# Gate times up on GpSimd instead of VectorE, with the rounding of h later in ScalarE's order

## The chip, the cores and the metric

The kernel runs on one core of one Trainium2 chip. The metric is the device time of one execution in microseconds. A core has TensorE (PE in the profile; its weight loads are PEld), VectorE (DVE), ScalarE (ACT), GpSimd (POOL) and SyncE (SP), which issues most DMAs. Each engine takes its own instructions in order; between engines they wait on semaphores.

## The reference

x is 2048 rows by 576 columns. After a layer norm, two branches work on the same normed rows and are multiplied:

```python
xn = _layernorm(x, axis=-1)
s = _A_ref(xn, A_wqkv, A_wo)              # attention with 32 heads of 18 columns, times wo
g = jnp.einsum("bsd,df->bsf", x, w_gate)  # in _B_ref, with xn for x; f has 4608 columns
u = jnp.einsum("bsd,df->bsf", x, w_up)
h = g * u
return jnp.einsum("bsf,fd->bsd", h, w_down)
return x + s * silu(B)                    # the end of reference(): B is that last product
```

## The kernel before, in words

All matrices are float32. A value that goes into a matmul is split into a rounded part (fp32r) and the rest, and a product is made of three matmuls (high by high, low by high, high by low). The split is two instructions: ScalarE copies the value with rounding, and GpSimd subtracts the rounded part from it.

A first stage (about 195 us) norms the rows and makes queries, keys and values. The main stage (about 195 to 2501 us) runs attention and the gated unit side by side. The last stage multiplies the two branches and applies wo.

In the main stage the gated unit's work is cut into 72 units: 4 blocks of 512 rows by 18 blocks of 256 columns of f. A unit has two halves j, so n = 2u + j counts 144 halves. TensorE runs two streams at once on the two halves of its rows: stream 0 makes up of half n (27 matmuls of 512 columns, L678), stream 1 makes gate of half n. Both accumulate in one of the four PSUM banks called pg. Up's end (`up_end`, L683) is a ScalarE copy of the bank to the tile `us`, of which there are two buffers. Gate's end (`gate_end`, L685 to L697) multiplies on VectorE the gate's bank with `us`, in place (L690), asks for the weights of half n + 2, rounds the product on ScalarE (L693) and subtracts on GpSimd (L694); this fills the tile `hs`. `turn_round` (L710) swaps the halves of `hs` into `hx` by two DMAs, issued by SyncE at the end of the unit before. Then the unit is multiplied with w_down (L720, 96 matmuls of 288 columns), and VectorE adds the banks to sums (L748).

Attention is put between these matmuls. An `a` item (L596) is a matmul of scores into one of two banks pa, of which VectorE takes row maxima (L598); there are 64 of them a head. After the 64th, VectorE folds the maxima and turns them (L604 to L613: `max_fold`, `max_rows`), and GpSimd issues four DMAs with them (L618), which stand in GpSimd's order ahead of whatever is put in later. A `b` item (L628) is the matmul of transposed scores into one of two banks pb, followed by an exponential on ScalarE (L630). Every seven row blocks there is a `visit`, in which TensorE does only the products with the values (L639, some 6 us). When a head is complete, `finish` (L651 to L659) divides: VectorE transposes into the tile `tp` (one buffer), scales it (L655) and transposes back, and GpSimd issues four DMAs with the result.

The order of all instructions is made when the program is built, by a planner written into the kernel (`order`, from L1100 on): it keeps a clock for each TensorE stream, and one "free from" time for VectorE, ScalarE and GpSimd, and puts in the item whose bank is free and whose goal is due. `engine(name, start, taken)` books time on an engine. GpSimd's DMA issues are not booked. For the end of a gate the planner books VectorE for 0.60 us, then ScalarE for 0.535 and GpSimd for 1.29.

Of the kernel before, what the change touches and what calls it, by code (L numbers as in the profile page):

```python
# [20 lines left out]
FT = mybir.dt.float32  # L21
FR = mybir.dt.float32r
I32 = mybir.dt.int32
AF = mybir.ActivationFunctionType
OP = mybir.AluOpType
# [15 lines left out]
def kernel(  # L41
# [10 lines left out]
    nc = tc.nc  # L52
# [116 lines left out]
    def g_get(n):  # L169

        if n == 2 * len(units):
            u = n // 2 - 1
            dw[u] = wpool.tile([128, 2, 2, 2, HALF], FR, name="wdl", tag="wgu", bufs=2)
            nc.sync.dma_start(dw[u].bitcast(FT), swd[columns_of(u)])
            ddone.add(u)
        if n >= 2 * len(units):
            return
        f = 2 * columns_of(n // 2) + n % 2
        if n > 1 and n // 2 % NF2 == 0:
            gw[n] = gw[n - 2]  # L180
            gdone.add(n)
            return
        w = gw[n] = g_tile()
        if n >= 2 * NF2:
            nc.sync.dma_start(w.bitcast(FT), swg[f])
            gdone.add(n)
            return
        if n not in graw:
            ready(gdone, n - 2)
        raw = graw.pop(n)  # L190

        def piece(b):
            nc.scalar.activation(w[:, b:b + 3, :], raw[:, b:b + 3, :], AF.Copy)  # L193
            nc.gpsimd.tensor_tensor(w[:, 9 + b:12 + b, :], raw[:, b:b + 3, :], w[:, b:b + 3, :].bitcast(FT),  # L194
                                    op=OP.subtract)

        def end():
            gdone.add(n)
            nc.sync.dma_start(swg[f], w.bitcast(FT))
            g_load(n + 2)  # L200

        chores.extend([(piece, (b,)) for b in (0, 3, 6)] + [(end, ())])
# [353 lines left out]
    n = 8  # L556
# [21 lines left out]
    with ExitStack() as mid:  # L578
# [106 lines left out]
        def gate_end(n, ps):  # L685
            u, j = divmod(n, 2)
            if j == 0:
                hs[u] = gp.tile([128, 2, 2, 512], FR, name="hs", bufs=2)
            h32 = us.pop(n)
            nc.vector.tensor_tensor(h32, ps, h32, op=OP.mult)  # L690
            g_get(n + 2)
            hj = hs[u][:, j]
            nc.scalar.activation(hj[:, 0, :], h32, AF.Copy)  # L693
            nc.gpsimd.tensor_tensor(hj[:, 1, :], h32, hj[:, 0, :].bitcast(FT), op=OP.subtract)  # L694
            if u == 0 and j or u == len(units) - 1:
                turn_round(u, j)

        hx = {}

        def turn_round(u, j):  # L700

            if u == len(units) - 1:
                if j == 0:
                    hx[u] = accp.tile([128, 2, 2, 512], FR, name="hxl", tag="acc")
                js = slice(j, j + 1)
            else:
                hx[u] = gp.tile([128, 2, 2, 512], FR, name="hx", bufs=1)
                js = slice(0, 2)
            for r in range(2):
                nc.sync.dma_start(hx[u][half[r], js].bitcast(FT), hs[u][half[1 - r], js].bitcast(FT))  # L710
# [2 lines left out]

        def down_start(r, u):
            ready(ddone, u)
            return bank("g", 1, slots[r])

        def down_op(r, u, s, ps, n):
# [129 lines left out]
        def stream(r):  # L848

            for u in range(len(units) + 1):  # L850
                for n in (2 * u, 2 * u + 1):
                    if u == len(units):
                        break
                    c, q = units[u]
                    box = []
                    for k in range(len(TERMS)):
                        def work(n=n, k=k, box=box, c=c, q=q):
                            if k == 0:
                                box.append(gu_start(r, n))
                            gu_op(r, n, box[0], k)  # L860
                            if q == NF2 - 1 and n % 2 and k % 3 == 2 and c < NCH - 1:
                                x_block(c + 1, k // 3, (64 * r,))
                                there["x", c + 1, k // 3, r] = moved(clk[r] + 0.5, 0.262)
                            if k == len(TERMS) - 1:
                                (gate_end if r else up_end)(n, box[0])
                                if r and n == 2 * len(units) - 1:
                                    wo_load()
                                    moved(max(clk), 1.47)
                        end = (("DVE", 0.60) if r else ("ACT", 0.50)) if k == len(TERMS) - 1 else None
                        yield LONG, k == 0, work, end, ("g", n, k)  # L870
                for s in range(4):
                    if not u:
                        break
                    box = []
                    for k in range(len(DTERMS)):
                        def work(s=s, k=k, box=box, u=u - 1):
                            if k == 0:
                                box.append(down_start(r, u))
                            down_op(r, u, s, box[0], k)
                            if k == len(DTERMS) - 1:  # L880
                                down_end(r, u, s, box[0])
                        end = ("DVE", 0.365) if k == len(DTERMS) - 1 else None
                        yield SHORT, k == 0, work, end, ("d", u - 1, 12 * s + k)
# [227 lines left out]
        def order():  # L1111
# [4 lines left out]
            wait = None  # L1116
            while any(heads) or na < TOTAL or nb < TOTAL or due:
                now = max(clk)
                small(now)
                if nb == TOTAL and not lo:  # L1120
                    begin()
# [28 lines left out]
                if can and (at <= clk[r] + 0.01 and (goal <= clk[r] or blocked) or op is None and (at <= clk[r] or not held)):  # L1150
                    clk[r] = max(clk[r], at)
                    score(r)
                elif op is not None:
                    length, first, work, end, (kind, n, k) = op
                    if first:
                        clk[r] = max(clk[r], next_free("g"))
                        slots[r] = banks["g"].index(next_free("g"))
                        banks["g"][slots[r]] = 1e9
                    work()
                    lands = issue(r, length)  # L1160
                    gone[r] += length
                    if end:
                        done = engine(end[0], lands, end[1])
                        banks["g"][slots[r]] = done + EARLY
                        if kind == "d":
                            if k == 47:
                                parts.setdefault(n, []).append(clk[r])
                                if len(parts[n]) == 2:
                                    downed[n] = moved(max(parts[n]) + 0.3, 1.18) if (n + 1) % NF2 and n + 2 < len(units) else 0.0
                                    if n + 2 < len(units):  # L1170
                                        there["h", n + 1] = moved(max(parts[n]) + 1.0, 1.05)
                        elif r == 0:
                            upped[n] = done
                        else:
                            gated[n] = done
                            fin = engine("ACT", done + 0.05, 0.535)
                            fin = engine("POOL", fin + 0.05, 1.29)
                            loaded[n] = moved(done - 0.4, 1.18) if (n // 2 + 1) % NF2 else 0.0
                            if n // 2 == len(units) - 1:
                                there["h", n // 2] = moved(fin, 0.524)  # L1180
                            elif n == 1:
                                there["h", 0] = moved(fin, 1.05)
                            for _ in range(2):
                                hot = n + 2 >= 2 * NF2 and n % (2 * NF2) in (34, 35, 0) and n + 2 < 2 * len(units)
                                for want in stacks:
                                    if hot and (want[0] is load_pair or n % (2 * NF2) == 2 * NF2 - 1):
                                        continue
                                    stacks.remove(want)
                                    send(want, fin + 1.4)
                                    break  # L1190
                    heads[r] = next(feeds[r], None)
                else:
                    clk[r] = max(clk[r] + 0.05, min(clk[1 - r] + 0.01, clk[r] + 0.3))
# [120 lines left out]
```

## Time and profile before

| | |
|---|---|
| median of 3 runs | 2570.12 us (2569.12 to 2572.28) |
| the profiled execution | 2571.43 us, of which its span is 2569.4 us |
| TensorE busy | 2547.8 us, 99% of the span |
| VectorE busy | 1933.2 us, 75% |
| ScalarE busy | 1467.1 us, 57% |
| GpSimd busy | 594.8 us, 23% |
| chain that ended last | 95% TensorE, 3% DMA, 1% VectorE |

The span runs from the first to the last instruction; the 2.0 us beyond it lie around the program. The chain is followed back from the last instruction, at each step to what released it. Times are microseconds unless marked as ns.

### The profile page before, as it was taken

Reading aid. Unit: us, or ns where it says so; the run is one execution under the profiler, and the core shown is the slowest. Engines: PE = TensorE matmul, PEld = TensorE weight load, DVE = VectorE, ACT = ScalarE, POOL = GpSimd, SP = SyncE. Lnnn points to the kernel's source line nnn. Section 1 sums busy time; section 2 is a strip of 40 time slices with the busy share of each in tenths; the row PEclk is TensorE's granted clock in tenths of the full one; section 3 lists DMA queues with packets and bytes.
Section 4 is the critical chain, followed back from the end, with each engine's and each line's share of the span. In section 5 each row is a group of like instructions: output and inputs, shape, how many; then the busy total and the mean of one; then the engine's idle time right before and its main releaser. Section 6 shows DMA issues by size and latency. Waiting matters only on the chain.

```text
span 2569.4 us, 59203 instructions
## 1 busy us (share of the span) xinstructions
PE 2547.8 (99%) x24360; PEld 2111.1 (82%) x24360; DVE 1933.2 (75%) x3377; ACT 1467.1 (57%) x2688; POOL 594.8 (23%) x663
## 2 busy tenths in 40 slices
PE   8999999999999999999999999999999999999999
PEld 7899888878878888877888888777888877888878
DVE  6208778777778898777778888777888887778437
ACT  5222666666756665555665665555665655556651
POOL 3214434434421111111111111111111111111125
PEclk9999999999999999999999999999999999999999
DMA  7799988888886666665686656665686666654567
GB/s 243 235 284 278 263 226 225 232 225 220 221 206 186 176 182 177 175 179 155 179 197 173 179 175 184 176 170 154 179 204 166 180 184 176 175 174 146 159 189 248
DMA packets 195898, 504.58 MB, mean 196 GB/s; under 512 B 58112, under 2 KB 116352, under 8 KB 156588
## 3 DMA queue, kind: packets, MB, share of 16 engines
q1 hardware_dynamic: 185676, 489.05, 68.6%
q0 software_dynamic: 9952, 11.74, 1.7%
q8 instruction: 192, 3.15, 0.6%
q14 instruction: 78, 0.64, 0.1%
HBM read 312.21 MB, written 107.61 MB: 163 GB/s over the span
## 4 chain that ended last, share of the span: by engine, by line
PE 95%; DMA 3%; DVE 1%; SPq 0%; ACT 0%; issue 0%; POOL 0%; ACTq 0%; DVEq 0%
PE pg L678 34%; PE pg L639 18%; PE pg L720 16%; PE pa L596 12%; PE pb L628 8%; PE pg L402 2%; PE pa L348 2%; PE pb L348 2%; PE pg L1244 1%; DMA hx<-hs 1%; PE pb L1244 1%; PE pa L1244 1%; DMA sqk<-hl 0%; DMA ring<-sqk 0%; DMA xc<-sx 0%; DMA o<-sot 0%
## 5 line engine op out<-in xcount | busy, mean ns | idle before, releaser
L598 DVE TENSOR_REDUCE mx<-pa 128x1 f32<-128x512 f32 x2048 | 1367.1, 686 | 223.6 <-PE pa L596 104.8
L630 ACT ACTIVATE pt<-pb 128x512 f32<-128x512 f32 x2048 | 1161.9, 598 | 534.8 <-PE pb L628 465.5
L678 PE MATMUL pg<-xc,wgu 64*128 64x512 f32 x7776 | 1366.1, 388 | 0.7 <-DMA xc<-sx 0.5
L678 PEld LDWEIGHTS pg<-xc,wgu 64*128 64x128 f32 x7776 | 1051.7, 184 | 41.6 <-DMA xc<-sx 1.2
L628 PE MATMUL pb<-pair,ring 64*128 64x512 f32 x1997 | 777.4, 395 | 1.5 <-DMA ring<-sqk 1.5
L596 PE MATMUL pa<-pair,ring 64*128 64x512 f32 x2006 | 776.9, 393 | 1.8 <-DVE mx L598 1.8
L720 PE MATMUL pg<-wd,hs 64*128 64x288 f32 x3408 | 523.4, 292 | 0.0
L720 PE MATMUL pg<-wd,hx 64*128 64x288 f32 x3408 | 515.2, 292 | 2.4 <-DMA hx<-hs 2.4
L694 POOL TENSOR_TENSOR hs<-us,hs 128x512 fp32r<-128x512 f32 x144 | 186.2, 1293 | 1320.3 <-ACT hs L693 1285.6
L720 PEld LDWEIGHTS pg<-wd,hs 64*128 64x128 f32 x3408 | 459.8, 185 | 4.0 <-DVE acc L748 0.2
L720 PEld LDWEIGHTS pg<-wd,hx 64*128 64x128 f32 x3408 | 453.4, 185 | 6.5 <-DMA hx<-hs 3.0
L639 PE MATMUL pg<-pt,vt 128*32 128x512 f32 x4096 | 454.8, 594 | 0.7 <-DVE acc L748 0.6
L596 PEld LDWEIGHTS pa<-pair,ring 64*128 64x128 f32 x2006 | 364.3, 184 | 69.8 <-issue 52.8
L628 PEld LDWEIGHTS pb<-pair,ring 64*128 64x128 f32 x1997 | 362.5, 184 | 8.7 <-issue 1.9
L639 PEld LDWEIGHTS pg<-pt,vt 128*32 128x32 f32 x4096 | 125.5, 110 | 284.0 <-issue 278.9
L748 DVE TENSOR_TENSOR acc<-acc,pg 128x288 f32<-128x288 f32 x544 | 233.0, 443 | 22.4 <-PE pg L720 21.4
L645 DVE TENSOR_TENSOR oc<-oc,pg 128x512 f32<-128x512 f32 x69 | 47.1, 683 | 220.4 <-PE pg L639 213.7
L693 ACT ACTIVATE hs<-us 128x512 fp32r<-128x512 f32 x144 | 91.0, 632 | 151.0 <-DVE us L690 149.7
L194 POOL TENSOR_TENSOR wgu<-wraw,wgu 128x384 fp32r<-128x384 f32 x108 | 108.6, 1017 | 97.1 <-ACT wgu L193 84.6
L643 ACT ACTIVATE oc<-pg 128x512 f32<-128x512 f32 x32 | 19.2, 598 | 185.0 <-PE pg L639 179.0
L690 DVE TENSOR_TENSOR us<-pg,us 128x512 f32<-128x512 f32 x144 | 98.2, 682 | 26.9 <-PE pg L678 15.7
L618 POOL DMA_DIRECT2D pair<-mt x128 | 77.8, 613 | 166.4 <-DVE mt L613 162.3
(141 smaller groups left out, 1359.0 us busy)
## 6 DMA issues: line engine op xcount, KB each, us to landing
wgu<-swg SPq DMA_DIRECT2D x102, 1152.0 KB
hx<-hs SPq DMA_DIRECT2D x142, 512.0 KB
wd<-swd SPq DMA_DIRECT2D x50, 1152.0 KB
swg<-wgu SPq DMA_DIRECT2D x36, 1152.0 KB
pair<-sqk SPq DMA_DIRECT2D x192, 144.0 KB
ring<-sqk SPq DMA_DIRECT2D x384, 72.0 KB
swd<-wd SPq DMA_DIRECT2D x18, 1152.0 KB
sqk<-hl SPq DMA_DIRECT2D x32, 512.0 KB
```

Source lines behind the costliest of these rows:

```text
L194: nc.gpsimd.tensor_tensor(w[:, 9 + b:12 + b, :], raw[:, b:b + 3, :], w[:, b:b + 3, :].bitcast(FT), op=OP.subtract)
L348: nc.tensor.matmul(p, wq[b, a], xcs[c][:, e, :], start=n == 0, stop=n == len(PAIRS) - 1)
L596: nc.tensor.matmul(p, q[rows, t * 128:(t + 1) * 128], k[rows, c * 512:(c + 1) * 512], start=True, stop=True)
L598: nc.vector.tensor_reduce(mx[h][:, t, c:c + 1], p, axis=AX.X, op=OP.max)
L628: nc.tensor.matmul(p, k[rows, t * 128:(t + 1) * 128], q[rows, c * 512:(c + 1) * 512], start=True, stop=True)
L630: nc.scalar.activation(pt[t, c], p, AF.Exp, scale=scale)
L639: nc.tensor.matmul(p[32 * c:32 * c + 32, :], vt[h // 2][:, t, 6 * (h % 2):6 * (h % 2) + 32], pt[t, c], start=t == ts[0], stop=t == ts[-1])
L678: nc.tensor.matmul(ps, gw[n][half[r], a, :], xg[i][half[r], e, :], start=k == 0, stop=k == len(TERMS) - 1)
L690: nc.vector.tensor_tensor(h32, ps, h32, op=OP.mult)
L694: nc.gpsimd.tensor_tensor(hj[:, 1, :], h32, hj[:, 0, :].bitcast(FT), op=OP.subtract)
L720: nc.tensor.matmul(ps[:, 0:HALF], (hx if k else hs)[u][half[r], j, a, s * 128:(s + 1) * 128], dw[u][half[r], k, j, e, :], start=n == 0, st ...
L748: nc.vector.tensor_tensor(a, a, ps[:, 0:HALF], op=OP.add)
```

## The change

For 132 of the 144 halves (`by_pool`: 8 <= n < 140, and not after the attention has ended) the product of gate and up is no longer one VectorE instruction. ScalarE copies the gate's bank to a tile `gs`, which shares the single buffer of `tp`; GpSimd multiplies `us` by `gs` in place. The two instructions of the split of h move to `h_split`. It is not put in at once but kept in a list, `halves`, with the time of the gate's end plus 2.6 us. The planner puts it in when that time has come, GpSimd will be free within 0.2 us and ScalarE within 0.3 us by its books. `settle` puts it in at the latest ahead of `turn_round` of its unit. The planner books the gate's end on ScalarE (0.50 us) instead of VectorE and the product on GpSimd (1.25 us). The time `fin`, from which loads of keys and queries may be sent, is the end of the product plus 2.0 us in place of the end of the subtraction.

```diff
             h32 = us.pop(n)
-            nc.vector.tensor_tensor(h32, ps, h32, op=OP.mult)
+            if by_pool(n):
+                gs = mp.tile([128, 512], FT, name="gs", tag="tp", bufs=1)
+                nc.scalar.activation(gs, ps, AF.Copy)
+                nc.gpsimd.tensor_tensor(h32, h32, gs, op=OP.mult)
+            else:
+                nc.vector.tensor_tensor(h32, ps, h32, op=OP.mult)
             g_get(n + 2)
+            if by_pool(n):
+                halves.append((max(clk) + 2.6, n, h32))
+            else:
+                h_split(n, h32)
+
+        halves = []
+
+        def by_pool(n):
+            return 8 <= n < 2 * len(units) - 4 and not fin
+
+        def h_split(n, h32):
+            u, j = divmod(n, 2)
             hj = hs[u][:, j]
             nc.scalar.activation(hj[:, 0, :], h32, AF.Copy)
             nc.gpsimd.tensor_tensor(hj[:, 1, :], h32, hj[:, 0, :].bitcast(FT), op=OP.subtract)
...
+        def settle(u):
+            while halves and halves[0][1] <= 2 * u + 1:
+                h_split(*halves.pop(0)[1:])
+
         def turn_round(u, j):
+            if u < len(units) - 1:
+                settle(u)
...
-                        end = (("DVE", 0.60) if r else ("ACT", 0.50)) if k == len(TERMS) - 1 else None
+                        end = (("DVE", 0.60) if r and not by_pool(n) else ("ACT", 0.50)) if k == len(TERMS) - 1 else None
...
+                if halves and halves[0][0] <= now and free["POOL"] <= now + 0.2 and free["ACT"] <= now + 0.3:
+                    h_split(*halves.pop(0)[1:])
+                    engine("POOL", engine("ACT", now, 0.535) + 0.05, 1.29)
...
-                            fin = engine("ACT", done + 0.05, 0.535)
-                            fin = engine("POOL", fin + 0.05, 1.29)
+                            if by_pool(n):
+                                fin = engine("POOL", done + 0.05, 1.25) + 2.0
+                            else:
+                                fin = engine("ACT", done + 0.05, 0.535)
+                                fin = engine("POOL", fin + 0.05, 1.29)
```

## Rows read from the trace of the kernel before

**Rows 1.** The page's busy times: engine, busy us, share of the span, instructions.

```profile
PE 2547.8 (99%) x24360; PEld 2111.1 (82%) x24360; DVE 1933.2 (75%) x3377; ACT 1467.1 (57%) x2688; POOL 594.8 (23%) x663
```

**Rows 2.** Busy times by stretch, 294 to 2430 us: stretch, length, engines, granted clock, DMA.

```profile
294.00:700.00 406.00, 405.80 (x4036) 330.23 (x4034) 315.00 (x551) 274.24 (x527) 167.86 (x169) 1.00 0.87 228
...
sum 2136.00, PE 2131.99 PEld 1740.48 DVE 1710.88 ACT 1305.72 POOL 452.25; mean PE 426.40 PEld 348.10 DVE 342.18 ACT 261.14 POOL 90.45
```

**Rows 3.** Waits of TensorE, 294 to 2430 us: waiter, releaser, total us, times, longest.

```profile
PE pb L628 <- DMA ring<-sqk: 1.5, 1, 1.5
PE pa L596 <- DVE mx L598: 1.0, 2, 0.5
PEld pa L596 <- DVE mx L598: 2.5, 4, 0.9
PEld pb L628 <- ACT pt L630: 0.8, 4, 0.2
```

**Rows 4.** Groups of instructions, 294 to 2430 us: count, busy us, mean ns, idle before.

```profile
L690 DVE TENSOR_TENSOR us<-pg,us 128x512 f32<-128x512 f32 x132 | 90.0, 682 | 8.1 <-PE pg L678 7.5
L683 ACT ACTIVATE us<-pg 128x512 f32<-128x512 f32 x131 | 78.3, 598 | 6.1 <-PE pg L678 3.8 <-PE pb L628 0.6
L693 ACT ACTIVATE hs<-us 128x512 fp32r<-128x512 f32 x132 | 83.4, 632 | 125.1 <-DVE us L690 123.9 <-DMA hx<-hs 0.6 <-DMA ring<-sqk 0.6
L694 POOL TENSOR_TENSOR hs<-us,hs 128x512 fp32r<-128x512 f32 x132 | 170.6, 1293 | 1220.8 <-ACT hs L693 1192.4 <-DMA ring<-sqk 15.1 <-DMA draw<-in_B_w_down_dram 7.8
```

**Rows 5.** Timeline of a head's end, 1014 to 1022 us: start, us, engine, operation.

```profile
1015.38 0.68 DVE L690 TENSOR_TENSOR us<-pg,us 128x512 f32<-128x512 f32 x1
1016.81 1.29 POOL L694 TENSOR_TENSOR hs<-us,hs 128x512 fp32r<-128x512 f32 x1 [11.82 <-ACT hs L693]
1016.95 1.18 DVE L610 TENSOR_SCALAR mm<-m 128x16 fp32r<-128x16 f32 x1
1019.22 0.50 PE L596 MATMUL pa<-pair,ring 64*128 64x512 f32 x1 [0.51 <-DVE mx L598]
```

**Rows 6.** L610's shortest, median, longest in ns; its first and last long instance.

```profile
L610 DVE TENSOR_SCALAR mm<-m x32: 174/174/1187, 247.6 to 2405.9; 128x16 fp32r<-128x16 f32 x32
...
462.84 0.59 DVE L610 TENSOR_SCALAR mm<-m 128x16 fp32r<-128x16 f32 x1
...
2055.36 1.19 DVE L610 TENSOR_SCALAR mm<-m 128x16 fp32r<-128x16 f32 x1
```

**Rows 7.** Timelines of GpSimd behind a head's end: first, middle and last case.

```profile
390.03 2.38 POOL L618 DMA_DIRECT2D pair<-mt  x4 [4.43 <-DVE mt L613]
390.22 0.68 DVE L690 TENSOR_TENSOR us<-pg,us 128x512 f32<-128x512 f32 x1
...
1503.86 0.66 DVE L690 TENSOR_TENSOR us<-pg,us 128x512 f32<-128x512 f32 x1
1504.23 2.44 POOL L618 DMA_DIRECT2D pair<-mt  x4 [13.88 <-DVE mt L613]
...
2198.00 2.44 POOL L618 DMA_DIRECT2D pair<-mt  x4 [9.66 <-DVE mt L613]
2198.56 0.68 DVE L690 TENSOR_TENSOR us<-pg,us 128x512 f32<-128x512 f32 x1
```

**Rows 8.** Timeline of pb's matmuls and exponentials, 1503 to 1507 us.

```profile
1503.00 0.39 PE L628 MATMUL pb<-pair,ring 64*128 64x512 f32 x1
1505.09 1.07 ACT L630 ACTIVATE pt<-pb 128x512 f32<-128x512 f32 x2
1505.94 0.39 PE L628 MATMUL pb<-pair,ring 64*128 64x512 f32 x1
1506.37 1.09 ACT L630 ACTIVATE pt<-pb 128x512 f32<-128x512 f32 x2 [0.21 <-PE pb L628]
```

**Rows 9.** Timeline of the unit with least time between subtraction and turn.

```profile
2200.45 1.29 POOL L694 TENSOR_TENSOR hs<-us,hs 128x512 fp32r<-128x512 f32 x1
2206.43 1.11 SPq L710 DMA_DIRECT2D hx<-hs  x2
```

More of the change, by code (lines that the diff above doesn't have):

```diff
@@ L715, in down_start @@
             ready(ddone, u)
+            settle(u)
             return bank("g", 1, slots[r])
```

## The prediction

> **What bounds the kernel now.** I read the page's busy times first: TensorE is busy 2547.8 of 2569.4 us, at 99%, against 75% for VectorE [rows 1]. The change acts only while halves 8 to 139 are made, and the 132 products that it moves all lie between 294 and 2430 us [rows 4]. So I cut the span by stretches: from 294 to 2430 us TensorE is busy 2131.99 of 2136.00 us idle for 4.0 us, and the granted clock in the stretches is 1.00, the higher of its two levels (2.4 GHz) [rows 2]. VectorE has 425 us free there (2136.00 less 1710.88), ScalarE 830. Neither is a bound in the sense of busy time; each matters only where TensorE comes to a bank that it has not yet emptied. The list of TensorE's waits prices that: 1.0 us of TensorE's idle time ended with VectorE's row maxima, 1.5 us with a DMA of keys, and the loads of weights ahead of an a item waited 2.5 us in four places for the maxima. For ScalarE's exponentials they waited 0.8 us in all [rows 3]. That is the whole of what a lighter VectorE can give back. Idle time is not all, since one of the two streams can stand while the other goes on, so I allow twice the idle time as the most that there is to win, 8 us.
>
> **What the change takes from VectorE.** 132 products of 682 ns, 90.0 us of busy time [rows 4]. In the middle of the stage they cost TensorE nothing, since the maxima behind them have their place in the order. They cost something at one kind of place. At 1015.38 us the product ran, the subtraction of that half held GpSimd from 1016.81 to 1018.10, and VectorE's tiny L610 took 1.18 us from 1016.95 on, ending when GpSimd ended. The next maxima stood behind it, and TensorE stood 0.51 us ahead of an a item at 1019.22 [rows 5]. L610 has a median of 174 ns and a longest of 1187 [rows 6]. There are three such long ones inside this stretch, the first at 462.84, the last at 2055.36 us [rows 6]; at all three a half's subtraction ran on GpSimd, and the waits of rows 3 for the maxima lie there. The loss at one such place is 0.9 us at most, by the longest wait of a weight load [rows 3]; I take 0.7, together 2.1 us.
>
> The Trainium skill has a rule for this, and it speaks against the change: "SBUF — State Buffer", section "Who interferes with whom", says that GpSimd and VectorE share a pair of ports, held for a whole instruction, and that a VectorE instruction of the tensor_scalar kind, or one with two operands in SBUF, waits until GpSimd's is done. Row and rule agree (1.18 us against 0.17). By the rule alone, without a look at where the locked instructions stand, more GpSimd work means more such waits, and never fewer.
>
> Now the count after the change. A half takes 16.2 us (2136 us over 132), and GpSimd's tensor work on it goes from one instruction of 1.29 us to two [rows 4], so a head's end meets one in 16% of the cases instead of 8%: of 31 head ends in place of about 2.5 (three were seen) about 5. The mean length of a block is half an instruction, 0.65 us, and what TensorE loses is less by about 0.3, as at the three seen. Without the product's 0.68 us in VectorE's queue at the same place I take 0.4 us each, 2.0 us in all against 2.1 now. The term is **0.0 us**; its bounds are -2.1 (no such place is left) and 5 x 0.9 - 2.1 = +2.4. The scaling in `finish`, which has two operands in SBUF, stands in visits, where TensorE needs no maxima: nothing.
>
> **What it adds to ScalarE.** 132 copies from a bank, at 598 ns by the same copy of up's bank [rows 4], 78.9 us, which lie in the 830 us that ScalarE has free. The copy empties the gate's bank in 0.6 us instead of 0.68, and two of the four pg banks are in use by the streams, so the bank is nobody's wait. What goes away on ScalarE is the stand ahead of L693: 123.9 us before 132 roundings, 0.94 us each, in which the exponentials queue behind it [rows 4]. TensorE's order was made knowing it, and TensorE waited 0.8 us for exponentials altogether [rows 3], so its end gives at most **0.8 us**; I count nothing.
>
> **What it adds to GpSimd.** 132 products; by the subtraction of the same shape 1293 ns each, 170.7 us, in the 1684 us that GpSimd has free (2136.00 less 452.25) [rows 2, 4]. The product has two operands like the subtraction, so between bounds of 0.6 us (half) and 1.3 I take the subtraction's. Early on GpSimd also splits the weights: from 294 to 700 us it is busy 167.86 of 406 us, and 25 products raise that by 32 us to half [rows 2]. The planner books both; free.
>
> **Where the planner's books are wrong.** Rounding is put into ScalarE's order 2.6 us after the gate's end at the earliest. Matmul to copy takes some 0.4 us (an item's start to the start of what reads it, 1505.94 to 1506.37 [rows 8]), the copy 0.6, the product 1.29, the hand-overs 0.1: the product is there at 2.4 us. But GpSimd's queue is in order, and the four DMA issues of a head's end, 2.44 us together [rows 7], are not booked. Where a half ends just behind a head, the product stands behind them, and ScalarE stands at the rounding, with all exponentials behind it, at a place where TensorE's order does not know it. Today only the subtraction waits there, and nobody waits for it soon. I looked for products that come behind a head's last a item and would be ready (0.75 us after L690's start) ahead of the end of the four issues: there are 8 in the stretch, the first at 390.22 us (ready 390.97, issues done 392.41: 1.44 late), the middle one 1503.86 (2.06 late), the last 2198.56 (1.13 late) [rows 7]; the eight come to 10.7 us. What of such a delay reaches TensorE? An item takes the bank of the item two before it. The item at 1505.94 takes that of 1503.00, whose exponential, the first of the two from 1505.09 on, ended at about 1505.63 (half of 1.07): 0.3 us to spare [rows 8]. Items follow each other by about 0.9 us, so the first exponential behind a rounding comes on average 0.45 us later, and 0.2 us lie between 2.4 and 2.6. A delay of 1.34 us (10.7 over 8) leaves 1.34 - 0.3 - 0.45 - 0.2 = 0.4 us: 8 x 0.4, about **+3 us**. Bounds: 0, as the wait of 0.94 us at every half costs nothing today [rows 3, 4], and 10.7 + 8 x 0.2 (the copy can start earlier than L690 did) = +12. I take the value nearer the lower end since the rows of a stand at this very place are there.
>
> **What is moved.** The split comes 1.5 to 3 us later. The turn of `hs` by SyncE stands behind it: the least time from the end of a subtraction (2201.74) to the issue of its turn (2206.43) is 4.7 us [rows 9], so SyncE's queue, with the loads of keys and weights behind the turn, does not stand longer. `settle` puts the rounding in ahead of the turn at the latest. The buffer of `us` is taken again two halves later, over 15 us. `gs` shares a buffer with `tp`: a gate's copy can wait for a `finish`, or a `finish` for a product, up to 2.5 us, but `finish` lies in visits, ahead of which VectorE has nothing of TensorE's next items. **0 us**, bound +1. That planned times of loads move by 1.3 us (`fin`) can make a wait like the 1.5 us for keys [rows 3] come or go: 0, from -2 to +3.
>
> **Sum.** The profiled execution took 2571.43 us, 1.3 more than the median of 2570.12; I forecast against the median. 0.0 (locks) + 3 (roundings) - 0.5 (half of the possible gain on ScalarE, rounded) + 0 = +2.5: **2572.5 us**, inside the 0.2% (5.1 us) that a measurement of this kernel can tell from no change. Its own range is 2567 to 2575.
>
> **Rivals.** *ScalarE held by late products, slower.* As above, but nearly the whole delay reaches TensorE because the items come in dense rows behind a head's end: 8 x 1.2, about +10, 2580 us. It decides from 5.1 us on, that is if the eight lose 0.65 us each. For it: ScalarE is in order, and the spare of a bank is only 0.3 us [rows 8]. Against it: 0.8 us of waits now, with ScalarE standing at every half [rows 3, 4]. 0.19.
> *The lock, slower.* More GpSimd instructions hit L610, or L611 behind it, than the 5 of the count, since two of them now follow a gate. To be slower by 5.1 us it takes (5.1 + 2.1) / 0.9 = 8 of 31 head ends at the highest price; at ten, 10 x 0.9 - 2.1 = +7, 2577 us. For it: rows 5. Against it: 8 is far from 5 when all must be the dearest. By the skill's rule above this would be the way the time goes. 0.05.
> *VectorE's relief, faster.* All three head ends, ScalarE's 0.8 us and the wait for keys go, and the streams' one-sided stands with them: 2.1 + 0.8 + 1.5 + 2, about -6, 2564 us. For it: each is seen once. Against it: it needs all of them, and nothing new. 0.06.
> *The product isn't moved, or the splits fall back to the turn.* Then TensorE's waits stay as they are, 2570 us; it counts with no change, 0.02.
>
> **How the numbers follow.** The forecast has 0.68 and the last rival 0.02: no change 0.70; slower 0.19 + 0.05 = 0.24; faster 0.06. The range leaves out half of the faster case and about a third of the slower cases: 2566 to 2580.
>
> **What would show it.** L690 falls to 12 instructions, a ScalarE copy of a gate's bank to `gs` of about 0.6 us and a GpSimd product of about 1.29 us come in 132 times; VectorE's busy time falls by 90 us, ScalarE's rises by 79, GpSimd's by 171; TensorE's stays within 3 us of 2547.8. ScalarE's waits ahead of the rounding change their releaser from VectorE to GpSimd, and only those behind a head's end are long. L610 has about five long instances. The prediction is wrong if TensorE waits over 5 us for exponentials, if the turn waits for GpSimd, or if the products run other than 1.3 us.

## The result and the profile after

The changed kernel takes 2575.61 us in the median of 22 runs, the kernel before 2571.77 in as many beside it: a ratio of 1.0015, with a 95% interval of 1.0009 to 1.0022. That is 3.8 us slower, and within the 5.1 us that the prediction took for no change. The forecast was +2.4 us against the median shown then. As will be seen, the sum came out near the truth because a loss twice as large as counted met gains that were not counted.

The profiled execution took 2575.07 us with a span of 2573.3. Its busy times, to be read beside [rows 1]:

```profile
PE 2544.1 (99%) x24360; PEld 2106.5 (82%) x24360; DVE 1871.6 (73%) x3245; ACT 1526.7 (59%) x2820; POOL 766.0 (30%) x795
```

The work was moved as told: VectorE has 132 instructions fewer, ScalarE and GpSimd 132 more. VectorE's busy time fell by 62 us and not by 90, and ScalarE's rose by 60 and not by 79: busy time is a union, and instructions that follow each other closely overlap at their ends, so one that is taken out or put in counts for less than its own length (the lengths of VectorE's instructions, added up, fell by 84 us). GpSimd's rose by 171.

The groups of the gate's end, from 294 to 2434 us (columns as in [rows 4]):

```profile
L693 POOL TENSOR_TENSOR us<-us,gs 128x512 f32<-128x512 f32 x132 | 172.2, 1305 | 978.0 <-ACT gs L692 958.3 <-DMA swd<-wd 8.3 <-DMA draw<-in_B_w_down_dram 8.2
L711 POOL TENSOR_TENSOR hs<-us,hs 128x512 fp32r<-128x512 f32 x132 | 170.4, 1291 | 185.7 <-ACT hs L710 177.4 <-PE pa L596 2.7 <-PE pg L678 2.5
L710 ACT ACTIVATE hs<-us 128x512 fp32r<-128x512 f32 x132 | 82.8, 627 | 16.7 <-POOL us L693 16.6
L692 ACT ACTIVATE gs<-pg 128x512 f32<-128x512 f32 x131 | 78.4, 598 | 7.4 <-PE pg L678 1.8 <-PE pa L596 0.2 <-PE pg L744 0.2
```

The product takes 1305 ns on GpSimd (682 on VectorE before), the copy 598. ScalarE's stand ahead of the rounding is 16.7 us instead of 125.1 [rows 4]: it is seven times smaller. But see who pays. These are the waits of TensorE in the same stretch, to be read beside [rows 3]:

```profile
PE pb L628 <- ACT pt L630: 5.2, 5, 1.5
PE pb L628 <- DMA ring<-sqk: 0.8, 1, 0.8
PE pa L596 <- DVE mx L598: 0.6, 1, 0.6
```

Waits for exponentials, which were no wait of TensorE's own before, are 5.2 us in five places; waits for row maxima fell from 1.0 to 0.6, those for keys from 1.5 to 0.8. Four of the five are 1.84, 1.84, 1.35 and 1.37 us from one matmul's start to the next, at 951.6, 1504.9, 1648.8 and 2202.0 us, each just behind a head's end. One of them in the timeline of the changed kernel (start, us, engine, operation, idle before and who ended it):

```profile
1501.11 0.59 ACT L692 ACTIVATE gs<-pg 128x512 f32<-128x512 f32 x1
...
1505.54 0.63 ACT L710 ACTIVATE hs<-us 128x512 fp32r<-128x512 f32 x1 [2.29 <-POOL us L693]
1506.08 1.76 ACT L630 ACTIVATE pt<-pb 128x512 f32<-128x512 f32 x3
...
1501.76 2.44 POOL L618 DMA_DIRECT2D pair<-mt  x4 [12.79 <-DVE mt L613]
1504.21 1.30 POOL L693 TENSOR_TENSOR us<-us,gs 128x512 f32<-128x512 f32 x1
...
1506.71 0.49 PE L628 MATMUL pb<-pair,ring 64*128 64x512 f32 x1 [1.45 <-ACT pt L630]
```

The gate's copy is done at 1501.70. The product could begin, but GpSimd is issuing the head's four DMAs until 1504.20. ScalarE comes to the rounding at 1503.26 and stands 2.29 us, three exponentials queue behind it, and TensorE stands for 1.45 us at a pb item. This is the half with the L690 at 1503.86 of [rows 7].

### The profile page after: what moved, and what is told of

Its sections match the earlier page's. It is cut to its first block, busy times and chain, and to the rows that moved or that the text cites. A ratio compares the mean times of both kernels' runs of the same rounds, so it can differ in the third digit from the quotient of the medians.

```text
span 2573.3 us, 59333 instructions
## 1 busy us (share of the span) xinstructions
PE 2544.1 (99%) x24360; PEld 2106.5 (82%) x24360; DVE 1871.6 (73%) x3245; ACT 1526.7 (59%) x2820; POOL 766.0 (30%) x795
## 4 chain that ended last, share of the span: by engine, by line
PE 94%; DMA 2%; DVE 2%; POOL 1%; SPq 1%; ACT 0%; issue 0%; ACTq 0%; DVEq 0%; POOLq 0%
PE pg L678 34%; PE pg L639 18%; PE pg L744 15%; PE pa L596 12%; PE pb L628 8%; PE pg L402 2%; PE pa L348 2%; PE pb L348 2%; PE pg L1274 1%; DVE mx L598 0%; DMA sqk<-hl 0%; PE pa L1274 0%; DMA hx<-hs 0%; PE pb L1274 0%; DMA ring<-sqk 0%; POOL pair L618 0%
## 5 line engine op out<-in xcount | busy, mean ns | idle before, releaser
L678 PEld LDWEIGHTS pg<-xc,wgu 64*128 64x128 f32 x7776 | 1035.9, 184 | 42.0 <-DVE acc L772 0.3
L693 POOL TENSOR_TENSOR us<-us,gs 128x512 f32<-128x512 f32 x132 | 172.2, 1305 | 978.0 <-ACT gs L692 958.3
```

The source lines that it names most:

```text
L678: nc.tensor.matmul(ps, gw[n][half[r], a, :], xg[i][half[r], e, :], start=k == 0, stop=k == len(TERMS) - 1)
L693: nc.gpsimd.tensor_tensor(h32, h32, gs, op=OP.mult)
```

## The experiments

Three questions: do late products hold ScalarE, and is that the loss; what does GpSimd's load on VectorE's port cost; and what does the later split do alone, as against the luck of a new order. Each ratio is to the kernel before on the same chip, with its 95% interval, from 11 runs of each kernel, but 22 of the change, four of e5 and five of c4.

| kernel | median us | ratio |
|---|---|---|
| the change | 2575.61 | 1.0015 (1.0009 to 1.0022) |
| the split 6.0 us after the gate (e1) | 2568.25 | 0.9986 (0.9977 to 0.9995) |
| GpSimd's DMA issues booked (e2) | 2567.89 | 0.9987 (0.9979 to 0.9996) |
| product on VectorE, split later (e3) | 2566.08 | 0.9982 (0.9973 to 0.9991) |
| before, subtraction twice (e4) | 2573.86 | 1.0011 (1.0002 to 1.0019) |
| product on GpSimd, split at once (e5) | 2593.34 | 1.0086 (1.0072 to 1.0100) |
| the change, DMAs of all head ends by SyncE (e6) | 2576.45 | 1.0021 (1.0012 to 1.0030) |
| before, loads counted 1.26 us later (e7) | 2571.40 | 0.9995 (0.9987 to 1.0004) |
| the change, DMAs of 31 head ends by SyncE (e9) | 2569.92 | 0.9989 (0.9981 to 0.9998) |
| before, product booked 0.66 (c1) | 2576.00 | 1.0013 (1.0004 to 1.0022) |
| the same with the split later (c3) | 2569.11 | 0.9994 (0.9985 to 1.0003) |
| before, pace 1.0045 (c2) | 2570.75 | 1.0001 (0.9992 to 1.0009) |
| the same with the split later (c4) | 2562.01 | 0.9962 (0.9948 to 0.9975) |

### The split still later

```diff
-                halves.append((max(clk) + 2.6, n, h32))
+                halves.append((max(clk) + 6.0, n, h32))
```

> The changed kernel, with the split of h put into ScalarE's order 6.0 us after the gate's end instead of 2.6. In the changed kernel TensorE stands at four places behind a head's end (951.6, 1504.9, 1648.8 and 2202.0 us; 1.84, 1.84, 1.35 and 1.37 us) for an exponential that stands behind a rounding whose product waits behind GpSimd's DMA issues. Theory 1 (ScalarE held by late products): a product that is up to 2.3 us late is there by 6.0 us, all four places go, 6 us less than the changed kernel, ratio to the kernel before 0.999 to 1.000, and the waits of pb's items for exponentials fall from 5.2 to under 1 us. Theory 2 (the new order, or the lock between GpSimd and VectorE, makes the loss): the ratio stays at 1.001 to 1.002. A turn of h that comes too late would show as waits of the matmuls with w_down for hx; the least time between a subtraction and its turn was 4.7 us before, so about 1 us is left, and none is expected.

Measured 0.9986. TensorE's waits for exponentials left its list altogether; from 294 to 2430 us it shows:

```profile
PE pb L628 <- DMA ring<-sqk: 1.4, 1, 1.4
PE pa L596 <- DVE mx L598: 0.3, 1, 0.3
PE pg L639 <- DVE acc L772: 0.3, 1, 0.3
```

7.4 us less than the change, a little more than the first theory's 6. But the order of TensorE is new in this kernel too, so it doesn't settle the cause alone.

### GpSimd's DMA issues booked

```diff
                 rows_done[h] = engine("DVE", 0.0, 0.85) + ROWS
+                engine("POOL", rows_done[h] - ROWS, 2.44)
```

> The changed kernel, with one line more in the planner: behind a head's end GpSimd is booked for the four DMA issues, 2.44 us. No instruction is added; only the order changes. Theory 1 (the loss is the planner's missing booking): a product behind a head's end is now booked late, its rounding is put in later, and exponentials are no longer behind it; the waits of pb's items for exponentials fall from 5.2 to under 1.5 us, ratio to the kernel before 0.999 to 1.0005. Theory 2 (reshuffled order or lock): 1.001 to 1.002 as for the changed kernel.

Measured 0.9987, and the waits for exponentials are 0.3 us in one place. One line of bookkeeping turns the change from 0.15% slower into 0.13% faster, though here too the order is new.

### The same order, without the issues ahead of the product

```diff
-                    nc.gpsimd.dma_start(rows, mt[32 * g:32 * g + 32, :])
+                    nc.sync.dma_start(rows, mt[32 * g:32 * g + 32, :])
```

> The changed kernel with the four DMAs of a head's end issued by SyncE instead of GpSimd. The order of TensorE, VectorE and ScalarE is the changed kernel's, instruction by instruction; only what stands ahead of a product in GpSimd's queue is gone. Theory 1 (products held by these issues hold ScalarE): the four places behind a head's end (1.84, 1.84, 1.35, 1.37 us) go, about 6 us less than the changed kernel, ratio to the kernel before 0.999 to 1.000. Theory 2 (the order itself, or the lock): 1.001 to 1.002 and the places stay. SyncE's queue now waits for VectorE at each head's end, some 2 to 4 us; loads behind it may come later, a wait for keys could grow.

The ratio, 1.0021, spoke for the second theory; the trace did not. Taking the start of each visit in both traces, this kernel gains on the change in four steps and nowhere else by more than 1.3: 1.9 us between the visits at 936 and 968 us, 1.9 between 1484 and 1515, 1.3 between 1636 and 1668, 1.4 between 2183 and 2215, which are the four places. At 2396 us it is 7.4 us ahead. Then the last head ends, whose maxima go to eight DMAs, and SyncE stands 15.8 us at them with the weights of w_down behind (SyncE's waits and TensorE's, 2400 to 2425 and 2405 to 2422 us):

```profile
SPq L618 <- DVE acc L772: 15.8, 1, 15.8
```

```profile
PE pg L744 <- DMA wd<-swd: 2.3, 1, 2.3
PE pg L744 <- DMA hx<-hs: 0.8, 1, 0.8
```

All but 0.9 us of the lead was lost there: 3.1 us in the two waits, and some 3.4 by a clock at half that followed the first of them (the last section shows it). A gain and a new wait had cancelled in the total. The profiled execution, 2572.79 us, was the fastest of the eleven; the others had lower mean clocks, down to 0.996, and no trace shows where. So the last head was left with GpSimd:

```diff
+                    (nc.gpsimd if h == H - 1 else nc.sync).dma_start(rows, mt[32 * g:32 * g + 32, :])
```

> The changed kernel with the DMAs of a head's end issued by SyncE for 31 heads; the last head's eight stay with GpSimd. The order of TensorE, VectorE and ScalarE is the changed kernel's. With all 32 on SyncE the profile was 7.4 us ahead of the changed kernel by 2396 us, in four steps at the four places, and lost 6.5 us at the last head's end to weights that stood behind SyncE's wait. Theory 1 (late products hold ScalarE): without the last head's part the lead stays: 5 to 7 us under the changed kernel, ratio to the kernel before 0.9985 to 0.9998. Theory 2 (the loss is elsewhere): 1.001 or more.

Measured 0.9989. The program gives TensorE, VectorE and ScalarE the change's order, instruction by instruction; from the visit at 936 us to that at 2215 (in the change's time) the kernel gains 6.7 us, in the same four steps. The place of 1504.9 us now reads (timeline of GpSimd and ScalarE):

```profile
1503.11 1.29 POOL L693 TENSOR_TENSOR us<-us,gs 128x512 f32<-128x512 f32 x1 [12.85 <-ACT gs L692]
...
1504.48 0.62 ACT L710 ACTIVATE hs<-us 128x512 fp32r<-128x512 f32 x1
1505.00 0.59 ACT L630 ACTIVATE pt<-pb 128x512 f32<-128x512 f32 x1
```

The product starts 0.08 us behind its copy, and the rounding has no wait. That the issues ahead of the product held ScalarE, and cost 6.4 us at four places, is shown.

### GpSimd's load alone

```diff
-            nc.gpsimd.tensor_tensor(hj[:, 1, :], h32, hj[:, 0, :].bitcast(FT), op=OP.subtract)
+            for _ in range(2 if 8 <= n < 140 else 1):
+                nc.gpsimd.tensor_tensor(hj[:, 1, :], h32, hj[:, 0, :].bitcast(FT), op=OP.subtract)
```

> The kernel before with GpSimd's subtraction done twice in the halves 8 to 139 (the same operands, the same result), without a booking, so that the order of all other instructions is that of the kernel before. It adds the 171 us of tensor work on GpSimd that the change adds, and no wait of ScalarE for it. Theory 'lock': GpSimd's instruction holds up VectorE's small instructions of a head's end (L610) more often, about 5 long ones of 31 instead of 3, each up to 0.9 us of TensorE's time: +1 to +3 us, ratio 1.0003 to 1.0012; were the lock the whole loss, 1.0015. Theory 'ScalarE held': the ratio is 1.000 within 0.0005, since nobody waits soon for the subtraction.

Measured 1.0011, inside what the lock was given, but the trace doesn't lay it there. The profiled execution was 2.5 us behind the kernel before already at the visit at 299 us, when one half had been doubled, and 2.5 behind at 2001 us. What lies there is a stretch with TensorE's clock at half (275 to 285 us; columns as in [rows 2], the granted clock third from the end):

```profile
275.00:285.00 10.00, 8.47 (x77) 8.47 (x79) 5.29 (x11) 4.75 (x10) 3.38 (x4) 0.66 0.84 257
```

In the profile of the kernel before, the clock of this stretch is 1.00. Eight of the eleven runs had a mean clock of 0.998, against three of 33 of the kernel before; the two with 1.000 took 2572.56 and 2573.80 us, where seven such runs of the kernel before have a median of 2570.44. Long L610 or L611 were in five head ends after 300 us in place of three, and one new gap of 0.7 us ahead of an a item came of it, at 533 us. So the lock's price is seen once, 0.7 us, and by the visit at 757 us, behind TensorE's wait for keys, 0.8 us of the distance are gone again. A clock at half between 259 and 285 us is in 11 of the 14 profiles of this study, 3.4 us long in nine and 6.8 us in e4 and e9; the kernel before and the change are two of the three without it. Why e4's clock was lower more often, in a stretch ahead of nearly all of the added work, is open, and so is the 0.11%.

### The later split alone, and new orders

The product back on VectorE, everything else of the change kept:

```diff
-            if by_pool(n):
-                gs = mp.tile([128, 512], FT, name="gs", tag="tp", bufs=1)
-                nc.scalar.activation(gs, ps, AF.Copy)
-                nc.gpsimd.tensor_tensor(h32, h32, gs, op=OP.mult)
-            else:
-                nc.vector.tensor_tensor(h32, ps, h32, op=OP.mult)
+            nc.vector.tensor_tensor(h32, ps, h32, op=OP.mult)
...
+                        end = (("DVE", 0.60) if r else ("ACT", 0.50)) if k == len(TERMS) - 1 else None
...
+                                fin = done + 3.34
```

> One part of the change alone: the product stays on VectorE as before, in the same halves, but the split of h is put in later as in the changed kernel (2.6 us after the gate's end at the earliest). ScalarE then doesn't stand 0.94 us ahead of each rounding. The prediction gave this stand at most 0.8 us of TensorE's time, so: ratio 0.999 to 1.0005; idle time of ScalarE ahead of the rounding released by VectorE falls from 124 to under 15 us; the three waits for row maxima next to a head's end (about 0.9 us each) stay or move. If the later rounding were itself the loss, the ratio would be 1.001 to 1.002.

Measured 0.9982: faster than both kernels, and faster than the range given. ScalarE's stand is gone and TensorE's list of waits is nearly empty (294 to 2430 us; the group of the rounding and the waits of TensorE):

```profile
L705 ACT ACTIVATE hs<-us 128x512 fp32r<-128x512 f32 x132 | 82.5, 625 | 0.3 <-DVE us L690 0.3
```

```profile
PE pg L639 <- DVE acc L767: 0.5, 2, 0.3
PE pa L596 <- DVE mx L598: 0.2, 1, 0.2
PE pg L739 <- DVE acc L767: 0.2, 1, 0.2
```

But a new order of the planner could do that by luck. One thing that the change also does to the order, counting the loads behind a half later, was tried by itself:

```diff
                             fin = engine("POOL", fin + 0.05, 1.29)
+                            if 8 <= n < 2 * len(units) - 4:
+                                fin += 1.26
```

> The kernel before with the one other thing that the change does to the planner: loads of keys and queries that are sent behind a half are counted 1.26 us later (halves 8 to 139). The split and the product stand as before. If this is what made the waits of 748 and 754 us smaller (2.8 us in all): ratio 0.9985 to 0.9995 and the wait of a pb item for a DMA of keys falls from 1.5 us to under 0.7; otherwise 1.000 within 0.0007 and the wait stays.

0.9995, with an interval that takes in 1; the wait for keys is 1.3 us instead of 1.5: no. Then two new orders of the kernel before, made by one number each (0.60 to 0.66 us for the product's booking; 1.005 to 1.0045 for the pace):

> The kernel before with one number of the planner changed: the product on VectorE is booked with 0.66 us instead of 0.60 (it takes 0.68). No instruction is added or taken, the split stands where it stood; only the order comes out anew. It asks how much of the 0.18% by which the later split was faster is the luck of an order. If the split's place is the cause: 1.000 within 0.001, no side favoured. If a new order alone gives such gains (the waits for keys and for row maxima at 748, 754, 1018 and 2056 us, together some 4 us, fall elsewhere or nowhere): 0.998 to 0.999.

> A second new order of the kernel before: the pace of the attention's items is 1.0045 in place of 1.005. Same question as with the other new order. If the split's place is the cause of the gain: 1.000 within 0.001. If a new order alone does it: 0.998 to 0.999. The waits of TensorE ahead of pa's and pb's items by name say which of the four places are left.

1.0013 and 1.0001. A new order alone moves this kernel by nearly as much as the change did, and neither of the two gained. The same two numbers with the split later:

> The product on VectorE and the split later (0.9982 against the kernel before), with the product booked at 0.66 us, as in the first new order of the kernel before (1.0013). If the later split gives its gain in any order: 0.997 to 0.9995, that is 0.1 to 0.4% under that order without the later split. If the gain was an order's luck: 0.999 to 1.002, no clear side against 1.0013.

> The product on VectorE and the split later, with the pace 1.0045, as in the second new order of the kernel before (1.0001). If the later split gives its gain in any order: 0.9975 to 0.9992. If the gain was an order's luck: 0.9995 to 1.0015. With the other pair that makes three pairs of the same planner's numbers with and without the later split.

0.9994 and 0.9962. So there are three pairs that differ by the split's place: 1.0000 and 0.9982, 1.0013 and 0.9994, 1.0001 and 0.9962. The later split wins in all three, by 0.18, 0.19 and 0.39%, 5 to 9 us. Adding up TensorE's named waits from 294 to 2430 us gives 4.0 and 0.9 us in the first pair, 4.1 and 1.3 in the second, 4.6 and 2.7 in the third: less in each, but only part of the gain. The waits that go are not of one kind: for keys and for row maxima in the first pair, for the weights of w_down (GpSimd and ScalarE) in the second, for x and row maxima in the third. Waits for exponentials are 0.9 us at most in each of the six.

Where the gain lies can be read from the starts of the visits. In each pair one step holds 3.6 to 4.2 us of it, where the partner with the split at once waits for a load: 3.9 us by the visit at 757 us in the first (the kernel before waits there 0.5 us for x and 1.5 for keys), 4.2 by 576 in the second (c1 waits 1.4 us for the split of w_down's weights, and its clock falls to half for 3.4 us), 3.6 by 758 in the third (c2 waits 1.9 us for x and 0.3 for keys). But c1, a new order without the later split, gains the 3.9 us at 757 too. TensorE from 724 to 760 us in the kernel before, in e3 and in c1:

```profile
724.00:760.00 36.00, 33.98 (x335) 25.59 (x331) 25.85 (x48) 19.80 (x35) 9.92 (x12) 1.00 0.96 210
724.00:760.00 36.00, 36.00 (x360) 25.80 (x359) 25.23 (x47) 19.38 (x34) 9.93 (x12) 1.00 0.88 200
724.00:760.00 36.00, 36.00 (x359) 29.97 (x355) 28.63 (x53) 22.17 (x40) 11.21 (x13) 1.00 0.99 232
```

And in the third pair 7.9 of the 10.0 us between the two profiles lie behind the last visit, at 2481 us, when the halves that differ are done: in c4 the last matmul of up or gate ends at 2480, in c2 at 2491. So three orders with the later split are faster than three without it, but that the split's place is the cause is not shown. The fastest kernel of the study is c4, 0.38% under the kernel before; 5.8 of the 7.0 us between those two profiles lie behind the last visit, too.

### The product on GpSimd, split at once

```diff
-                halves.append((max(clk) + 2.6, n, h32))
+                h_split(n, h32)
...
-                                fin = engine("POOL", done + 0.05, 1.25) + 2.0
+                                fin = engine("POOL", done + 0.05, 1.25)
+                                fin = engine("ACT", fin + 0.05, 0.535)
+                                fin = engine("POOL", fin + 0.05, 1.29)
```

> One part of the change alone: the product on GpSimd, but the split put into ScalarE's order at once behind the copy, and booked so (ScalarE is booked from the product's end). ScalarE then stands at every rounding for the product of 1.3 us and the hand-overs, some 1.4 us 132 times (185 us of stand, in a stretch where ScalarE has some 750 us free), instead of 0.94 us for VectorE before. If a stand that the planner books is free, as the prediction read from the kernel before: the ratio is that of a new order, 0.999 to 1.0015, with waits for exponentials behind head's ends as in the changed kernel (the four DMA issues are still not booked), 4 to 8 us. If the stand itself costs (the later split is what makes things faster): 1.002 to 1.005.

1.0086, beyond both expectations. Its group of the rounding and its waits of TensorE, 294 to 2455 us:

```profile
L710 ACT ACTIVATE hs<-us 128x512 fp32r<-128x512 f32 x132 | 83.4, 632 | 207.3 <-POOL us L693 200.6 <-DMA wgu<-swg 5.3 <-DMA hx<-hs 1.4
```

```profile
PE pb L628 <- ACT pt L630: 15.5, 8, 3.4
```

ScalarE stands 207 us, 1.6 us a half where 1.4 were expected, and TensorE waits 15.5 us for exponentials in eight places. In all eight the product stands behind the four DMA issues of a head's end, and ScalarE 2.2 to 5.3 us at the rounding. At the other 124 halves it stands 1.42 us in the mean, 176.5 us together, and TensorE waits for no exponential. So the first expectation had the mechanism and not the size. Whether the stand that the planner books costs anything besides is open: from the first visit to the last this kernel loses 31 us on the kernel before, more than the waits and what follows them explain, and the end of its order gives 11 back. Five of the eight waits are followed by a fall of the clock, as in these two stretches at a head's end:

```profile
1024.00:1028.70 4.70, 2.61 (x25) 2.00 (x22) 2.10 (x4) 2.44 (x5) 3.39 (x4) 1.00 0.82 250
1028.70:1032.20 3.50, 3.50 (x25) 3.46 (x23) 1.97 (x5) 1.98 (x5) 0.00 (x0) 0.51 0.10 24
```

## Why the prediction was right, and where its terms were not

*What bounds the kernel.* Right: TensorE stayed at 99%, and nothing that VectorE was relieved of is seen to come back as time. With the DMA issues booked or out of the way the product on GpSimd gives 0.9987 or 0.9989, on VectorE 0.9982; the intervals overlap, and the orders differ. The 90 us taken from VectorE are worth nothing that could be measured.

*Where the planner's books are wrong.* The mechanism, the place and four of the eight halves were right: 951.6, 1504.9, 1648.8 and 2202.0 us are the halves named behind the products of 951.8, 1503.86, 1646.5 and 2198.56 us before. The size was not. The term that was mis-sized is "8 x 0.4, about +3 us": four of the eight cost nothing and four cost 1.3 to 1.9, 6.4 us together, inside the bounds of 0 and 12. The mean delay of 1.34 us less a mean spare was no model of it: at 1504 us the stand was 2.29 us, three exponentials were queued behind it, and 1.45 us of that reached TensorE. A stand as long behind another of the eight, that of 390.22 us before, cost nothing: it lay in a visit, and TensorE's next pb item came at 395.52 us (timeline of the changed kernel).

```profile
389.37 6.22 PE L639 MATMUL pg<-pt,vt 128*32 128x512 f32 x56
392.61 0.63 ACT L710 ACTIVATE hs<-us 128x512 fp32r<-128x512 f32 x1 [2.43 <-POOL us L693]
395.52 0.50 PE L628 MATMUL pb<-pair,ring 64*128 64x512 f32 x1
```

So it matters whether pb items follow the stand. The prediction had also named waits for exponentials of over 5 us as a sign that it is wrong. They came to 5.2: the total held, the size of this term did not.

*What it adds to ScalarE.* The text gives the stand's end "at most 0.8 us" and counts nothing, while the sum takes off 0.5. The three pairs, 5 to 9 us, seem to speak against it; but most of each lies at loads and at the end of the order, and in e5 a booked stand of 1.42 us at 124 halves cost no named wait. So whether the stand's end is worth more than 0.8 us stays open. What the visits of the two profiles show is this: the change is 0.7 us ahead at 299 us, loses 6.4 at the four places and gains 4.5 elsewhere up to 2424 us, 2.5 of them in the step to 757, where TensorE's waits for x and keys fell from 2.0 to 0.8 us. That is the "come or go" of a load's wait, which the prediction put at 0, from -2 to +3. From 2424 us to the end it loses 2.7 us (below). So 3.4 us more loss than counted at the four places, 4 us more gain elsewhere, and 2 us at the two ends nearly cancel: that the sum was within 1.4 us of the measured 3.8 is in part luck.

*The lock.* Of the 31 head ends behind the first, three met a long L610 (461.5, 1225.0 and 2055.7 us: 0.45, 0.50 and 1.02 us), not five. The tile's shortest, median and longest, beside [rows 6]:

```profile
L610 DVE TENSOR_SCALAR mm<-m x32: 174/175/1024, 247.1 to 2407.5; 128x16 fp32r<-128x16 f32 x32
```

TensorE's waits for row maxima fell by 0.4 us [rows 3]. The term of 0.0 stands, within its bounds. The rule of the Trainium skill ("SBUF — State Buffer", "Who interferes with whom") is borne out as a mechanism, a long L610 coming while GpSimd works in this kernel as in the others; that more GpSimd work means more such waits was seen for the doubled subtraction, once, by 0.7 us, and not for the change.

*What is moved.* No wait of TensorE for hx came between 294 and 2434 us. The shared buffer cost VectorE 7.1 us at four `finish`es that waited for a product, in visits, with no wait of TensorE named behind it: free, as said. The wait for keys fell from 1.5 to 0.8 us.

*Not foreseen.* From the visit at 2424 us to that at 2450 the change loses 1.7 us with TensorE busy throughout in both kernels, and e6 and e9, which have its order, lose the same there. From the last visit to the end it loses another 0.9. There, up to 2492 us, TensorE waited 1.7 us for the last product on VectorE, which the change doesn't move and which stood behind a `finish`; e2, with an order of its own, waited 0.8 there. The cause is argued, not shown: the luck of the order, which the two new orders of the kernel before put at up to 0.13%. Of the signs, TensorE's busy time fell by 3.7 us and not by 3 at most, and VectorE's and ScalarE's moved by 62 and 60 us, not by 90 and 79.

*The rivals.* "ScalarE held by late products" is what happened, at two thirds of the 10 us it was given; that the whole stayed within 0.2% is owed to the gains elsewhere. "VectorE's relief" fell.

## What to carry to other kernels

When a product moves to another engine, look first at what that engine's queue holds that nobody booked: here four DMA issues of 0.6 us each, harmless as long as nobody waited behind them, cost 6.4 us once ScalarE did. Booking those issues, or putting the instruction that waits for the product later, took the waits away. Stands that the planner had booked, 1.42 us at 124 halves of e5, cost TensorE no wait by name; the stands that it had not booked did. And a gain of 0.2% in a planned kernel says little until the same planner has been run with other numbers: two harmless ones moved the time by 0.01 and 0.13%. Compare the starts of a recurring piece of work in both traces, too: it shows whether a gain lies where the change acts.

## What the runs showed of the hardware

After some longer idle times of TensorE the granted clock fell to half, 1.2 GHz. In the kernel with the split at once it did so behind five of its waits, each time for 3.4 us, as at 1028.7 us above, where TensorE had been busy for 2.61 of 4.70 us; these five waits were 1.9 to 3.4 us long. Behind another, of 2.76 us up to 470.55, it did not. In the changed kernel, waits of 1.45 us passed at a clock of 1.00. In e6 a wait of 2.3 us up to 2413.4 was followed by 6.8 us at half, in which another of 0.8 us lay:

```profile
2413.70:2420.60 6.90, 6.09 (x41) 5.75 (x39) 0.60 (x2) 1.99 (x4) 0.00 (x0) 0.51 0.84 248
```

So some waits cost more than their own length. Five stretches of 3.4 us at half speed, by estimate 1.7 us each, are 8.5 us; with the 15.5 us of waits that is 24 of the 31 us that this kernel loses on the kernel before from the first visit to the last.
